# Decoding 64-bit weights with a sign-carrying parametric Relu and two VectorE passes

## The chip, the cores and the metric

The kernel runs on one core of a Trainium2 chip. The core has a matrix engine (TensorE, in the profile PE, with its weight loads as PEld), a vector engine (VectorE, DVE), an activation engine (ScalarE, ACT), a general engine (GpSimd, POOL) and a queue that starts transfers (SyncE, SP). Each engine works through its own instructions in the order in which the program lists them; between engines, semaphores hold an instruction back until its inputs are there or its output buffer is free.

The metric is the device time of one execution in microseconds (us). Lower is better.

## What is computed

Causal attention with a decay, over 8 batches, 8 heads, 576 tokens and 64 features a head, and then a two-layer block with a layer norm over the 512 features of each token:

```python
scores = scale * q @ k^T                       # scale = 1/8
scores = where(causal, -1e9, scores + cum[:, :, :, None] - cum[:, :, None, :])
attn   = softmax(scores) ; x = (attn @ v)      # heads side by side: 512 features
xn     = (x - mean) / sqrt(var + 1e-6) * g_ln
out    = x + maximum(xn @ w_ch1, 0) @ w_ch2    # 512 -> 2048 -> 512
```

`cum` is the running sum of log(f). The two weight matrices arrive as 64-bit floating point, 512 x 2048 and 2048 x 512; all else is 32-bit. The kernel reads a weight's 64 bits as two 32-bit words and makes a 32-bit number of them on the chip.

## The kernel before

**Work on attention.** The 64 heads are taken one after the other, each in four units (slots `t` = 1 to 4), 256 units in all. A unit runs the product of queries and keys (`qk_mm`, L368 to L371), a fused mask and minimum on VectorE (L394), the exponential on ScalarE (L405), a sum's reciprocal on VectorE (L410, L411) and a scaling on GpSimd (L412). Two units later the probabilities are transposed on TensorE (L418) and copied out (L468, and L473 on VectorE); a unit after that they are multiplied with the values (`av_unit`, L481 for the first 16 heads, L503 later) and finished on ScalarE (L534, L537). The first 8 heads use plain 32-bit products; from head 8 on, a head's raw queries and keys come through one buffer `raw` (L319), are rounded on ScalarE (L337, L344) and have the rest subtracted on GpSimd (L340, L348).

**The two-layer block.** Tokens are taken in 18 chunks of 256, each in 16 steps. A step is 12 products for the first layer (`mm1`, L580 to L582), a Relu on ScalarE (L588), a rest on VectorE (L593), and 6 products for the second layer (`mm2`, L602 to L604). The first step may run from unit 35 on, when the tokens and the weights that it reads are there. Each weight is used as a rounded part and a remainder (`w1h`, `w1l`, `w2h`, `w2s`).

**The preparation of the weights** is the class `WPrep`, where the change lies. There are 32 items, alternately a 512 x 128 block of the first matrix and a 128 x 512 block of the second; each is 512 words of 64 bits in each of 128 partitions. A tick starts the next item and moves the earlier ones on by a step:

- `load` (L143): a transfer into `raw` (tile `wr`, three buffers). The high words `hw` are every second 32-bit word, the low words `lw` the others.
- `scaled` (L156): ScalarE reads the high word as a 32-bit float and multiplies it by 2^-112, so that its exponent fits after a shift to the left by three. The result is the tile `wy` (five buffers).
- `decode` (L165): three VectorE steps. L173 keeps the sign bit of the high word, in place. L174 shifts `wy` left by three and sets the sign. L177 shifts the low word right by 29 and sets its three bits in `wy`.
- `colsum` (L182, first layer only, two ticks later): eight products (L189) that sum over features, for the mean of the layer norm; `centre` (L191): four VectorE steps (L197), one tick after that, which apply `g_ln` and subtract the mean.
- `high` (L211): ScalarE rounds (L214); `low` (L216): GpSimd subtracts (L218) and so frees the `wy` buffer; `keep` (L220): the second layer's remainders go out to memory.

**What sets the order.** The order of all instructions is written out by hand. A unit runs the pieces named by the letters of a string, for units 0 to 36 `WwQsSthAeMrgFBmlLNPaRf`, for 37 to 69 `WwQSstAMhPelgLNFrfmBRa`. "W" calls `tick` if one is due: about every 2.4 units up to unit 34, then 0.95 a unit, so that the items are done at about unit 57. A tick first runs whatever VectorE steps are left in the queue (`fill(99)`), then issues the loads and the steps `high`, `keep` and `low` of earlier items, and then puts the new item's decode steps and an older item's centring steps into the queue in turn. The scaling of the next item is put at place 5 of the queue, or at its end if it is shorter. Letters "w", "g" and "f" take 1, 2 and 3 entries out of the queue. A tick with a first-layer item (even) has no centring; one with a second-layer item (odd) has four centring steps. "Q" is the product of queries and keys, "e" the exponential, "r" the Relu, "F" the finish copy, "P" the preparation of the next head, "M" and "N" the two layers, "s" the column sums.

Of the kernel before, what the change touches and what calls it, by code (L numbers as in the profile page):

```python
# [8 lines left out]
F32 = mybir.dt.float32  # L9
# [3 lines left out]
AF = mybir.ActivationFunctionType  # L13
ALU = mybir.AluOpType
# [44 lines left out]
def attn_moe(ctx: ExitStack, tc: tile.TileContext, qk, v, f, g, w1, w2, out):  # L59
    nc = tc.nc  # L60
# [14 lines left out]
    def m2(name, dt):  # L75
        return work.tile([P, 512], dt, tag="m2", bufs=11, name=name)
# [9 lines left out]
    for i in range(WARM):  # L86
# [4 lines left out]
        out=mask[:, S - P :], in_=mask[:, S - P :], pattern=[[-1, P]], base=0,  # L91
# [42 lines left out]
    class WPrep:  # L134
# [21 lines left out]
        def scaled(self, n):  # L156
            layer, j = self.items[n]
            d = self.d[n]
            if layer == 1 and self.tick_no < W_BORROW:
                d["y"] = m2(f"wy{layer}_{j}", U32)  # L160
            else:
                d["y"] = wpool.tile([P, DM], U32, tag="wy", bufs=W_FLOAT, name=f"wy{layer}_{j}")
            nc.scalar.activation(d["y"].bitcast(F32), d["hw"].bitcast(F32), AF.Copy, scale=2.0**-112)

        def decode(self, n):  # L165
            layer, j = self.items[n]
            d = self.d[n]
            y, z, low = d["y"], d["hw"], d["lw"]
            d["w"] = y.bitcast(F32)
            ve = nc.vector  # L170

            return [
                lambda: ve.tensor_scalar(out=z, in0=z, scalar1=0x80000000, scalar2=None, op0=ALU.bitwise_and),  # L173
                lambda: ve.scalar_tensor_tensor(  # L174
                    out=y, in0=y, scalar=3, in1=z, op0=ALU.logical_shift_left, op1=ALU.bitwise_or
                ),
                lambda: ve.scalar_tensor_tensor(  # L177
                    out=y, in0=low, scalar=29, in1=y, op0=ALU.logical_shift_right, op1=ALU.bitwise_or
                ),
            ]  # L180

# [483 lines left out]
    class Moe:  # L665
# [21 lines left out]
        low = []  # L687
# [211 lines left out]
```

## Time and profile before

| | us |
|---|---|
| three runs | 1252.57, 1253.7, 1260.37 |
| their median | 1253.7 |
| span of the profiled execution, first to last instruction | 1260.6 |
| TensorE busy in it | 1230.2 |
| VectorE busy in it | 782.8 |
| ScalarE busy in it | 645.2 |
| GpSimd busy in it | 426.8 |

The profile is one execution recorded by the hardware. Its page gives the busy time of each engine, the same in 40 equal slices of the span together with the granted clock of TensorE, the chain of work that ended last (followed back from the last instruction: what released each step), and groups of instructions by line and tile, with the mean time of one and the idle time of the engine ahead of them. Further views give windows of time, single instructions in order of time, and waits by pairs of lines. In a row, `wy<-wy,wr` means that the tile `wy` is written from `wy` and `wr`; "L177" is line 177. Idle time of an engine that does not set the end costs nothing.

### The profile page before, as it was taken

The page shows a single profiled execution, that of the slowest core. Times are in us where ns is not written, and L with a number is a line of the kernel's source. Part 1 is how long each engine was busy: PE and PEld are TensorE (multiplying, and loading weights), DVE is VectorE, ACT ScalarE, POOL GpSimd, SP SyncE. Part 2 cuts the span into 40 slices and gives each one's busy share as a digit, 9 for nine tenths or more (in the row PEclk, how much of TensorE's full clock was granted, in tenths as well). Part 3 has the DMA queues.
Part 4 walks back from the last instruction along what each step waited for, and adds up shares of the span by engine and source line. Part 5 has one row for each costly group of instructions (what it writes and reads, how often), then busy time and mean ns, then how long its engine had stood idle before and what let it go on. Part 6 is the DMA issues. An engine that isn't in the chain of part 4 may idle for free.

```text
span 1260.6 us, 25515 instructions
## 1 busy us (share of the span) xinstructions
PE 1230.2 (98%) x8148; PEld 1085.2 (86%) x8148; DVE 782.8 (62%) x2868; ACT 645.2 (51%) x1920; POOL 426.8 (34%) x529
## 2 busy tenths in 40 slices
PE   8997898999999999999999999999999999999998
PEld 5554686889999999999999999999999999999997
DVE  5587888357576768576767666666767673233232
ACT  5577666555555556565656555655555552112111
POOL 3356556333343334334443434343434330000000
PEclk7799899999999999999999999999999999999999
DMA  5366674544554545444545454545454534444432
GB/s 154 110 183 204 198 240 160 159 124 155 154 165 148 168 141 171 137 150 149 156 144 160 145 168 151 168 151 166 149 152 147 168 104 136 125 126 117 151 109 92
DMA packets 139381, 190.77 MB, mean 151 GB/s; under 512 B 32496, under 2 KB 81648, under 8 KB 139248
## 3 DMA queue, kind: packets, MB, share of 16 engines
q1 hardware_dynamic: 139248, 189.15, 49.0%
q8 instruction: 65, 1.06, 0.3%
q14 instruction: 68, 0.56, 0.1%
HBM read 157.46 MB, written 23.36 MB: 143 GB/s over the span
## 4 chain that ended last, share of the span: by engine, by line
PE 86%; DVE 5%; DMA 4%; ACT 1%; POOL 1%; issue 1%; SPq 0%; DVEq 0%; POOLq 0%; ACTq 0%
PE h L580 11%; PE h L581 10%; PE h L582 10%; PE acc L602 10%; PE acc L603 10%; PE acc L604 10%; PE tr L418 7%; PE o L503 5%; PE o L481 3%; PE s L370 3%; PE s L371 3%; DMA raw<-in_qk_dram 3%; PE s L368 1%; PE xp L418 1%; DVE wy L174 1%
## 5 line engine op out<-in xcount | busy, mean ns | idle before, releaser
L412 POOL TENSOR_SCALAR p<-p,st 64x64 f32<-64x64 f32 (+4 forms) x320 | 173.8, 546 | 568.1 <-DVE st L411 225.9
L580 PE MATMUL h<-x,w1h 128*128 128x256 f32 x1152 | 329.6, 286 | 0.0
L581 PE MATMUL h<-x,w1h 128*128 128x256 f32 x1152 | 325.9, 283 | 0.7 <-DVE x L565 0.7
L582 PE MATMUL h<-x,w1l 128*128 128x256 f32 x1152 | 324.9, 282 | 0.0
L588 ACT ACTIVATE hh<-h 128x256 fp32r<-128x256 f32 x288 | 110.4, 383 | 287.7 <-PE h L582 281.0
L593 DVE SCALAR_TENSOR_TENSOR hh<-h,hh 128x256 fp32r<-128x256 f32 x288 | 121.4, 422 | 193.3 <-ACT hh L588 189.0
L602 PE MATMUL acc<-w2h,hh 128*128 128x512 f32 x576 | 228.1, 396 | 0.0
L603 PE MATMUL acc<-w2s,hh 128*128 128x512 f32 x576 | 226.4, 393 | 0.0
L604 PE MATMUL acc<-w2h,hh 128*128 128x512 f32 x576 | 225.7, 392 | 0.0
L580 PEld LDWEIGHTS h<-x,w1h 128*128 128x128 f32 x1152 | 218.2, 189 | 5.2 <-issue 0.9
L581 PEld LDWEIGHTS h<-x,w1h 128*128 128x128 f32 x1152 | 218.2, 189 | 4.6 <-DVE x L565 1.3
L582 PEld LDWEIGHTS h<-x,w1l 128*128 128x128 f32 x1152 | 218.0, 189 | 0.0
L405 ACT ACTIVATE p<-p,st 64x64 f32<-64x64 f32 (+4 forms) x320 | 178.3, 558 | 60.8 <-DVE st L394 58.1
L468 ACT CAST ph<-tr 64x128 fp32r<-64x128 f32 (+4 forms) x384 | 108.6, 332 | 110.4 <-PE tr L418 82.6
L418 PE MATMUL tr<-identr,p 128*128 128x128 f32 (+1 forms) x896 | 143.7, 277 | 9.0 <-POOL p L412 4.7
L394 DVE CUSTOM_DVE_ANT_0 p<-s,mask 64x64 f32<-64x64 f32 (+4 forms) x320 | 130.3, 420 | 15.5 <-PE s L368 9.8
L418 PEld LDWEIGHTS tr<-identr,p 128*128 128x128 f32 (+1 forms) x896 | 102.9, 132 | 35.3 <-POOL p L412 9.1
L604 PEld LDWEIGHTS acc<-w2h,hh 128*128 128x128 f32 x576 | 108.2, 188 | 25.3
L473 DVE TENSOR_TENSOR ph<-tr,ph 64x192 fp32r<-64x192 f32 x192 | 57.8, 301 | 106.1 <-ACT ph L468 102.9
L602 PEld LDWEIGHTS acc<-w2h,hh 128*128 128x128 f32 x576 | 108.7, 189 | 13.4 <-issue 0.9
L603 PEld LDWEIGHTS acc<-w2s,hh 128*128 128x128 f32 x576 | 109.0, 189 | 12.3
L370 PE MATMUL s<-hi 128*64 128x64 f32 x336 | 109.8, 349 | 8.3 <-POOL hi L348 6.5
(81 smaller groups left out, 1848.4 us busy)
## 6 DMA issues: line engine op xcount, KB each, us to landing
w2s<-w2d SPq DMA_DIRECT2D x288, 256.0 KB
raw<-in_qk_dram SPq DMA_DIRECT2D x56, 576.0 KB
wr<-in_w_dram SPq DMA_DIRECT2D x32, 512.0 KB
vr<-in_v_dram SPq DMA_DIRECT2D x64, 160.0 KB
out_dram<-xt SPq DMA_DIRECT2D x36, 256.0 KB
xq<-hi SPq DMA_DIRECT2D x56, 144.0 KB
xa<-xs SPq DMA_DIRECT2D x32, 160.0 KB
w2d<-wl SPq DMA_DIRECT2D x16, 256.0 KB
```

The lines of the kernel that those rows point to most:

```text
L370: mm(sp, h.hi[:, 0, q0 : q0 + m], h.hi[:, 1, a:z], start=True, stop=False)
L394: nc.vector.tensor_tensor_reduce(out=pt[:m, a:z], in0=sp, in1=mask[:m, off + a : off + z], scale=-SCALE, scalar=3.0e38 if i == 0 else st[: ...
L405: nc.scalar.activation(pt[:m, :w], pt[:m, :w], AF.Exp, bias=st[:m, i : i + 1], scale=-1.0, accum_out=st[:m, 2:3])
L412: nc.gpsimd.tensor_scalar(out=pt[:m, :w], in0=pt[:m, :w], scalar1=st[:m, 3:4], scalar2=1.0, op0=ALU.mult, op1=ALU.mult)
L418: nc.tensor.transpose(out_, in_, ident[:m, :m])
L580: mm(ph, w1h[:, k, fs], c.x[k][:, 0, :], start=(k == 0), stop=False)
L581: mm(ph, w1h[:, k, fs], c.x[k][:, 1, :], start=False, stop=False)
L582: mm(ph, w1l[:, k, fs], c.x[k][:, 0, :], start=False, stop=(k == KT - 1))
L593: nc.vector.scalar_tensor_tensor(out=h[:, 1, :], in0=ph, scalar=0.0, in1=h[:, 0, :].bitcast(F32), op0=ALU.max, op1=ALU.subtract)
L602: mm(c.acc[i], h[:, 0, ts_], w2h[:, j, :], start=(j == 0), stop=False)
L603: mm(c.acc[i], h[:, 0, ts_], low, start=False, stop=False)
L604: mm(c.acc[i], h[:, 1, ts_], w2h[:, j, :], start=False, stop=(j == FT - 1))
```

## The change

ScalarE's scaling becomes a parametric Relu. For a positive high word it gives the same as before. For a negative one, the scaled value is multiplied by alpha = 2^32 as well, so the exponent is higher by 32. The shift to the left by three drops the sign bit and the two upper bits of the exponent, and the bit of the exponent worth 32 lands where the sign belongs: the sign is carried through. The mask of the sign (before L173) and its separate combining pass (before L174) go. The shift of the low word by 29 becomes a pass of its own, in place, and one pass shifts `wy` and combines. An item has two VectorE decode steps in place of three; the queue and its letters are unchanged, so the later entries move up by one.

```diff
-            nc.scalar.activation(d["y"].bitcast(F32), d["hw"].bitcast(F32), AF.Copy, scale=2.0**-112)
+            nc.scalar.activation(d["y"].bitcast(F32), d["hw"].bitcast(F32), AF.Prelu, scale=2.0**-112, alpha=2.0**32)
...
-            y, z, low = d["y"], d["hw"], d["lw"]
+            y, low = d["y"], d["lw"]
...
-                lambda: ve.tensor_scalar(out=z, in0=z, scalar1=0x80000000, scalar2=None, op0=ALU.bitwise_and),
+                lambda: ve.tensor_scalar(out=low, in0=low, scalar1=29, scalar2=None, op0=ALU.logical_shift_right),
                 lambda: ve.scalar_tensor_tensor(
-                    out=y, in0=y, scalar=3, in1=z, op0=ALU.logical_shift_left, op1=ALU.bitwise_or
-                ),
-                lambda: ve.scalar_tensor_tensor(
-                    out=y, in0=low, scalar=29, in1=y, op0=ALU.logical_shift_right, op1=ALU.bitwise_or
+                    out=y, in0=y, scalar=3, in1=low, op0=ALU.logical_shift_left, op1=ALU.bitwise_or
                 ),
```

## The prediction

> **What bounds the kernel now.** I read the head of the page first, then a table of busy times by stage, then the chain of the work that ended last, stage by stage, and last the waits and the timeline where the chain leaves TensorE.
>
> ```profile
> span 1260.6 us, 25515 instructions
> PE 1230.2 (98%) x8148; PEld 1085.2 (86%) x8148; DVE 782.8 (62%) x2868; ACT 645.2 (51%) x1920; POOL 426.8 (34%) x529
> ...
> PE   8997898999999999999999999999999999999998
> ...
> DVE  5587888357576768576767666666767673233232
> ...
> PEclk7799899999999999999999999999999999999999
> ...
> PE 86%; DVE 5%; DMA 4%; ACT 1%; POOL 1%; issue 1%; SPq 0%; DVEq 0%; POOLq 0%; ACTq 0%
> ```
>
> TensorE is busy 98% and carries 86% of the chain. Only in the first seven slices (31.5 us each) is its line or its clock below the rest, and there the DVE line is highest. The weights are decoded in just that time. The next view is a table of windows: for each stretch its length, then busy us (and instructions) of PE, PEld, DVE, ACT, POOL, then the granted clock, the DMA share and GB/s.
>
> ```profile
> 0.00:14.00 14.00, 9.01 (x45) 7.61 (x45) 9.07 (x20) 6.14 (x10) 5.74 (x15) 0.99 0.66 198
> 14.00:44.00 30.00, 29.97 (x88) 18.79 (x89) 14.74 (x56) 14.44 (x44) 8.17 (x13) 0.50 0.41 108
> 44.00:98.00 54.00, 50.77 (x249) 31.37 (x248) 40.30 (x151) 38.56 (x121) 26.05 (x32) 0.96 0.56 167
> 98.00:138.00 40.00, 27.12 (x138) 17.95 (x137) 29.85 (x84) 25.00 (x72) 25.89 (x26) 0.87 0.59 179
> 138.00:180.00 42.00, 42.00 (x275) 35.35 (x273) 38.46 (x98) 27.77 (x76) 24.39 (x23) 1.00 0.72 227
> 180.00:220.00 40.00, 35.71 (x225) 28.19 (x224) 32.39 (x108) 25.05 (x71) 23.19 (x25) 1.00 0.59 190
> 220.00:1260.00 1040.00, 1035.66 (x7139) 945.91 (x7138) 618.00 (x2358) 508.21 (x1527) 313.34 (x397) 1.00 0.48 146
> ```
>
> After 220 us TensorE idles 4.3 us in 1040: whatever is won earlier is kept there, and nothing more is won. In 138 to 180 it idles not at all, though DVE is busy 38.46 of 42 us. In 14 to 44 it is busy throughout at half the clock. What a lighter DVE can still take away is TensorE's idle time: 3.2 us in 44 to 98, 12.9 in 98 to 138 and 4.3 in 180 to 220, together 20.4 us, and some at the very start.
>
> **The change part by part.** The rows by form give count, busy us, mean ns, and idle time ahead.
>
> ```profile
> L163 ACT ACTIVATE wy<-wr 128x512 f32<-128x512 f32 x32 | 21.5, 671 | 8.3 <-POOL w1l L218 3.6 <-DMA wr<-in_w_dram 2.7 <-POOL wl L218 1.9
> ...
> L173 DVE TENSOR_SCALAR wr<-wr 128x512 uint32<-128x512 uint32 x32 | 16.9, 528 | 0.8 <-ACT wy L163 0.8
> ...
> L174 DVE SCALAR_TENSOR_TENSOR wy<-wy,wr 128x512 uint32<-128x512 uint32 x32 | 35.3, 1103 | 0.0
> ...
> L177 DVE SCALAR_TENSOR_TENSOR wy<-wr,wy 128x512 uint32<-128x512 uint32 x32 | 30.2, 945 | 0.6
> ```
>
> (a) *The scaling* stays one ACTIVATE on the same 512 words. No Prelu is in this trace. Nearest is the Copy that it replaces, 671 ns; a gain is excluded since the same words go through the same engine, and the far end is a reload of the activation table (a rival below). I take 671, so nothing. (b) *The mask of the sign* (L173) goes and *the shift of the low word* comes: one tensor_scalar in place on the other strided half of the same tile. I take the row of L173 for both, so nothing. It now waits for the load and no longer for ScalarE, and the load is one that the scaling of the same item awaited before it. (c) *One of two combining passes goes*: the new one has the shape and strides of L174, so L177's row is what is saved. 32 x 945 ns = 30.2 us of DVE, 35.3 us by L174's row.
>
> ```profile
> 115.60 1.41 POOL L340 TENSOR_TENSOR kl<-raw,hi 64x576 fp32r<-64x576 f32 x1
> ...
> 115.95 1.62 DVE L174 SCALAR_TENSOR_TENSOR wy<-wy,wr 128x512 uint32<-128x512 uint32 x1
> ...
> L177 DVE SCALAR_TENSOR_TENSOR wy<-wr,wy x32: 676/693/1807, 9.0 to 203.5; 128x512 uint32<-128x512 uint32 x32
> ```
>
> The third row has min, median and max: 676, 693 and 1807 ns. Two rows above, a pass that began 0.35 us after a POOL operation ended 0.56 us after it: the long ones lie beside POOL. That time may pass on to the pass that is left, so the low end is 32 x 676 ns = 21.6 us. I take the rows of the chain below for the path and these for the load. The Trainium skill says the same against the change: by "SBUF — State Buffer", the section "Who interferes with whom", a DVE operation with two SBUF inputs and a POOL operation that reads SBUF lock each other out for a whole instruction. By that rule the wait belongs to POOL's work and stays, and the saving is nearer 21.6 us than 30.2.
>
> What lies on the path: the lines of the chain in three of these stages.
>
> ```profile
> by line: PE o L481 13.3%; DMA raw<-in_qk_dram 10.8%; DVE wy L174 10.3%; DMA kl<-in_qk_dram 7.6%; DVE wy L177 6.8%; DVE p L394 6.6%; PE s L368 6.1%; ACT p L405 6.1%; POOL p L412 5.9%; issue 5.6%; PE tr L418 4.2%; POOL w1l L218 3.4%; DVE wr L
> ...
> by line: DMA raw<-in_qk_dram 39.0%; issue 13.1%; PE o L481 10.6%; POOL hi L348 7.6%; POOL p L412 5.7%; DVE x L565 4.2%; ACT ph L468 3.6%; POOL kl L340 3.5%; DVE wy L197 3.5%; ACT p L405 3.5%; DVE wy L177 3.1%; POOL w1l L218 2.3%; PE tr L418
> ...
> by line: DMA wr<-in_w_dram 13.3%; PE o L481 9.9%; DMA xr<-xb 9.2%; DVE wy L174 9.1%; DVE wr L173 8.1%; DVE wy L177 5.2%; DVE wy L197 4.2%; PE acc L602 3.5%; PE tr L418 3.5%; DVE p L394 3.4%; issue 2.9%; PE h L582 2.5%; PE h L580 2.5%; PE h
> ```
>
> L177 has 6.8% of 53 us (45 to 98) = 3.6 us, 3.1% of 39 us (98 to 137) = 1.2 us, and 5.2% of 38 us (180 to 218) = 2.0 us. The pieces of the chain in order of time (start, us, what) show it where it counts:
>
> ```profile
> 53.91 1.64 DVE wy L177
> ...
> 69.31 0.69 DVE wy L177
> ...
> 82.03 0.69 DVE wy L177
> ...
> 194.38 0.60 DVE wy L177
> ...
> 199.69 0.69 DVE wy L177
> ...
> 203.47 0.68 DVE wy L177
> ```
>
> TensorE idles only 3.2 us in the first stage, so between 0 and 3.2 I take three passes of 0.68 = 2.0 there: behind them TensorE's own matmuls are late next. In the third stage the three pieces are 1.97, under its 4.3 us of idle time. In the second the loads of raw, 39% of 39 us = 15.2 us, are late next. In 138 to 180, TensorE covers all of it; if that cover were gone, some 8 passes of 0.68 to 0.95 us would show.
>
> ```profile
> ACT w1h L214 <- DVE wy L197: 17.2, 9, 3.6
> ...
> PE s L370 <- POOL hi L348: 6.5, 2, 3.7
> ...
> PE tr L418 <- DVE wy L197: 4.1, 1, 4.1
> ```
>
> (Total us, times, longest.) (d) *The queue of VectorE steps gets shorter.* On ticks with a centring (odd), the steps were two decode steps each beside a centring step, the third, the scaling, and two centrings flushed at the next tick; now one is flushed. The rounding w1h at that next tick waits 17.2 us in 9 places for the last centring. One pass and one centring fewer ahead of it shorten some of these waits; off the path they cost nothing. Between 0 (ScalarE is not the bound) and 9 x 0.95 = 8.6 us, I take 0.8 us in 98 to 138 and 0.5 us in 180 to 220, near the low end, since ACT holds 1% of the chain.
>
> ```profile
> 9.88 2.11 PE L368 MATMUL s<-kl,xf 66*64 66x64 f32 x8 [1.36 <-DMA kl<-cumr]
> ...
> 12.15 0.69 DVE L177 SCALAR_TENSOR_TENSOR wy<-wr,wy 128x512 uint32<-128x512 uint32 x1
> ...
> 13.64 1.03 PE L418 MATMUL tr<-identr,p 128*64 128x128 f32 x3 [1.65 <-POOL p L412]
> ```
>
> (e) *The start.* L177 of item 1 stands ahead of the softmax's small VectorE steps; TensorE's wait of 1.65 us shortens by its 0.69 us, 0.7, and stage 14 to 44 begins that much sooner.
>
> (f) *The scaling of the next item moves forward on even ticks.* With two decode steps instead of three it leaves with fill "g" and not with "f", ahead of the finish copy and of the raw halves. No DMA is issued anew, and SP's order stays. It waits today 8.2 us in all (3.6 + 2.7 + 1.9 in its row above). Gain excluded: its result is needed a tick later; a loss up to a POOL subtraction on each of 16 ticks (rival). I take 0, as the seven waits there now are mostly under 1.2 us (8.2 / 7).
>
> **Sum**: 2.0 + 1.2 + 2.0 + 0.8 + 0.5 + 0.7 = 7.2 us off 1260.6, 0.57%. The profiled execution stands 0.55% above the median of the three runs, 1253.7, near the slowest, 1260.4. Off the median: 1246.5, say 1247.
>
> **The rivals.**
> *Hidden anyway.* TensorE is full in 14 to 44 and 138 to 180, and in 98 to 138 the loads of raw end last. Then only the 0.7 of the start and a little of 180 to 220 stay: about 1252. Against it stands DVE's unbroken part of the chain around 191 to 205 us.
>
> *The clock is kept.*
>
> ```profile
> 123.00:126.00 3.00, 3.00 (x11) 0.50 0.88 271
> ...
> 130.00:136.00 6.00, 4.09 (x11) 0.50 0.53 153
> ```
>
> (TensorE alone: length, busy, clock, DMA share, GB/s.) After gaps TensorE runs at half clock: 30 us after the two gaps at the start, 3 and 6 us later. If the shorter second gap keeps the clock up, stage 14 to 44 falls from TensorE's 30 us to DVE's: 14.74 us at the 75% load that DVE has in 44 to 98 (40.30 / 54) = 19.8 us. That saves 10 more: 1236. Against it: the first gap stays, and the gap left is still about 1 us. "TensorE: Matmul & The Clock Gate" of the Trainium skill, in Part 1, has the clock return after one busy window of about 3.4 us. The trace differs: 29.97 busy us at 0.50.
>
> *Slower, by the moved scaling.*
>
> ```profile
> L218 POOL TENSOR_TENSOR wl<-wy,w2h x16: 1265/1362/1701, 38.1 to 212.3; 128x512 fp32r<-128x512 f32 x16
> ```
>
> Each of 16 even ticks could hold ScalarE for the subtraction that frees the buffer, 16 x 1.36 = 21.8 us; less 7.2 that is +14.6: 1268. It decides only if nearly all reaches TensorE, 19.7 us of 21.8 for over 1%. For it: two waits on wl are there now. Against: ACT is idle 83 of the first 220 us.
>
> *Slower, by table reloads.*
>
> ```profile
> L114 ACT ACT_TABLE_LOAD x1 | 1.3, 1283 | 0.7 <-PEq L887 0.7
> L405 ACT ACT_TABLE_LOAD x1 | 1.3, 1283 | 0.0
> ```
>
> Two loads in all, at Ln and at the first Exp; Copy and Relu run between exponentials without one. If Prelu were not in the table of Exp, each item would need two: 64 x 1.283 = 82 us. ACT's 137 us up to 220 (the six rows above) become 219; at the 92% load that DVE reaches in 138 to 180 they need 238: +18, 1272. The Trainium skill, "ScalarE: Activation LUTs", section on table sets, puts cheap functions such as relu and copy in every set, without naming Prelu.
>
> **How the numbers follow.** Forecast 0.48, hidden 0.25, clock 0.20, moved scaling 0.04, tables 0.03. A measurement here tells about 1% (12.5 us) from no change. Faster by over 1%: the clock and 0.02 of the forecast's upper end, 0.22. Slower: the last two, 0.07. Within: 0.71. The range reaches from the clock's 1236 to 1257, above the hidden case by the spread of the runs; 0.07 above and some below are left out. The forecast's own range is 1241 to 1251.
>
> **What would show it.** Right: L177's group gone, 32 instructions fewer on DVE, DVE busy in 44 to 220 down by 18 to 28 us; two table loads; the scaling near 671 ns; TensorE idle in 180 to 220 under 2.5 us; the chain at 191 to 205 without 0.7 us per item. Wrong: stage 98 to 138 still 40 us long with DVE lighter (then raw's load is the bound); ScalarE's waits at the scaling well over 8.2 us; another clock in 14 to 44.

## The result and the profile after

The changed kernel takes 1248.17 us (median of 20 runs, 1241.18 to 1255.70) against 1254.32 us before (20 runs, 1250.38 to 1268.25). The ratio is 0.9936, with a 95% interval from 0.9911 to 0.996: some 5 to 11 us faster, 0.6%, inside the 1% that was called no change. The forecast was 1247.

The page of the changed kernel, head, slices and chain:

```profile
span 1241.2 us, 25467 instructions
PE 1221.9 (98%) x8148; PEld 1081.0 (87%) x8148; DVE 751.8 (61%) x2836; ACT 646.4 (52%) x1920; POOL 425.5 (34%) x529
...
PE   8998999999999999999999999999999999999998
...
DVE  5666676366676767676767586767667663233232
...
PEclk8997999999999999999999999999999999999999
...
PE 88%; DVE 3%; ACT 3%; DMA 2%; POOL 2%; issue 1%; SPq 1%; POOLq 0%; DVEq 0%; ACTq 0%
```

VectorE lost 32 instructions and 31.0 us of work (782.8 to 751.8) and holds 3% of the chain instead of 5%. The span is 19.4 us shorter, three times what the medians say. The table by stage (length, then busy us and instructions of PE, PEld, DVE, ACT, POOL, then granted clock, DMA share, GB/s) shows why:

```profile
0.00:14.00 14.00, 9.26 (x49) 7.70 (x50) 6.80 (x18) 6.26 (x10) 5.68 (x16) 0.93 0.67 195
14.00:44.00 30.00, 28.94 (x140) 18.36 (x138) 19.04 (x84) 22.16 (x70) 12.59 (x19) 0.92 0.64 173
44.00:98.00 54.00, 50.94 (x239) 31.96 (x239) 33.29 (x140) 38.76 (x123) 28.39 (x37) 0.90 0.60 180
98.00:138.00 40.00, 35.14 (x196) 27.24 (x196) 29.00 (x88) 27.48 (x77) 24.90 (x24) 0.88 0.67 209
138.00:180.00 42.00, 41.13 (x260) 33.18 (x258) 28.56 (x88) 27.06 (x73) 25.77 (x24) 1.00 0.71 229
180.00:220.00 40.00, 39.53 (x246) 31.36 (x245) 25.14 (x98) 25.72 (x79) 20.38 (x23) 1.00 0.55 175
```

In this execution the stage from 14 to 44 us ran at a clock of 0.92, with 140 matmuls done; the profiled execution before had 0.50 and 88. The two profiles differ in the change and in the clock, and cannot be subtracted. TensorE's idle time from 44 to 220 us fell from 20.4 to 9.3 us (3.06 + 4.86 + 0.87 + 0.47), in windows that no longer hold the same work: the last column sum, at 202.6 us before, is at 185.1 now.

**Runs at the same clock.** Each run of the changed kernel and of all that follow lists its time and its mean granted clock, and the two go together: in every kernel here runs with a lower mean clock tend to take longer. A line through the runs of all kernels below, with one slope and a level for each kernel, has a slope of 9.7 us for each 0.01 of clock and leaves a scatter of 1.9 us. Four runs with a mean clock under 0.965 are left out of it: three slow ones (1693.7 us at 0.654 in e5, 1695.4 at 0.652 in the kernel before, 1989.7 at 0.555 in e9) and one of e8, 1253.9 us at 0.938, which lies far off the line. The level at a clock of 0.988 compares kernels without that lottery: 1254.6 +- 0.4 us before (93 runs), 1247.6 +- 0.8 after, a difference of 7.1 +- 0.9.

The 93 runs of the kernel before are those beside the experiments, on three chips, with a level of 1254.5 to 1254.8 on each; the 20 beside the changed kernel list no clock. The level takes out whatever a change does through the clock itself. The mean clock was 0.986 before and 0.987 after, a difference of 0.0018 +- 0.0025, so a share of 1.7 +- 2.4 us by that way is neither shown nor excluded. The table gives this level beside medians and ratios; the ratio's interval holds the clock's scatter, the level's does not.

| kernel | runs | median us | ratio to before (95%) | mean clock | level at 0.988, us |
|---|---|---|---|---|---|
| changed | 20 | 1248.2 | 0.9936 (0.9911 to 0.996) | 0.987 | 1247.6 +- 0.8 |
| e1, parametric Relu alone | 12 | 1257.1 | 1.0011 (0.9981 to 1.0041) | 0.984 | 1254.6 +- 1.1 |
| e2, empty third entry | 8 | 1246.4 | 0.9924 (0.9893 to 0.9954) | 0.988 | 1247.5 +- 1.3 |
| e3, three passes in two entries | 12 | 1258.5 | 1.0022 (0.999 to 1.0055) | 0.981 | 1253.8 +- 1.1 |
| e4, pass put back | 12 | 1257.2 | 0.9995 (0.9968 to 1.0021) | 0.986 | 1254.8 +- 1.1 |
| e5, changed, start filled | 8 | 1247.4 | 0.9905 (0.9868 to 0.9941) | 0.989 | 1248.2 +- 1.4 |
| e6, before, start filled | 12 | 1256.0 | 0.9982 (0.9948 to 1.0016) | 0.988 | 1255.5 +- 1.1 |
| e7, changed, raw split | 9 | 1247.0 | 0.9906 (0.9869 to 0.9943) | 0.987 | 1245.9 +- 1.2 |
| e8, before, raw split | 12 | 1252.2 | 0.996 (0.9928 to 0.9991) | 0.987 | 1251.2 +- 1.1 |
| e9, changed, filled and split | 12 | 1245.4 | 0.9899 (0.9865 to 0.9934) | 0.990 | 1246.0 +- 1.1 |
| e10, pass back in items 0 to 12 | 12 | 1247.4 | 0.9948 (0.9917 to 0.998) | 0.988 | 1250.1 +- 1.1 |
| e11, pass back in items 13 to 19 | 12 | 1249.1 | 0.9937 (0.9903 to 0.997) | 0.988 | 1248.9 +- 1.1 |
| e12, pass back in items 20 to 31 | 12 | 1251.1 | 0.9961 (0.9934 to 0.9989) | 0.986 | 1249.1 +- 1.1 |

The mean clock is that of the runs on the line. Ratios are to the runs of the kernel before on the same chip, whose median was 1256.9 beside e1 to e4, 1257.6 beside e5 to e8 and 1254.9 beside e9 to e12.

The rows by form of the changed kernel (count, busy us, mean ns, idle time ahead) answer to those of the decode; the centring is now L194, the rounding L211, the subtraction L215, the load of raw L316 and its remainder L345:

```profile
L163 ACT ACTIVATE wy<-wr 128x512 f32<-128x512 f32 x32 | 21.4, 668 | 10.4 <-POOL w1l L215 3.5 <-POOL wl L215 3.4 <-DMA wr<-in_w_dram 3.3
...
L174 DVE SCALAR_TENSOR_TENSOR wy<-wy,wr 128x512 uint32<-128x512 uint32 x32 | 35.9, 1121 | 0.1
...
L173 DVE TENSOR_SCALAR wr<-wr 128x512 uint32<-128x512 uint32 x32 | 14.9, 464 | 0.0
```

The scaling costs what it did (668 ns after 671). The pass that stays is about as long as the like one before (1121 after 1103), and the one of 945 ns is gone. The shift of the low word takes 464 ns where the mask took 528.

### The profile page after: what moved, and what is told of

The parts are those of the page before. It is cut to its first block, busy times and chain, and to the rows that moved or that the text cites. A ratio compares the mean times of both kernels' runs of the same rounds, so it can differ in the third digit from the quotient of the medians.

```text
span 1241.2 us, 25467 instructions
## 1 busy us (share of the span) xinstructions
PE 1221.9 (98%) x8148; PEld 1081.0 (87%) x8148; DVE 751.8 (61%) x2836; ACT 646.4 (52%) x1920; POOL 425.5 (34%) x529
## 4 chain that ended last, share of the span: by engine, by line
PE 88%; DVE 3%; ACT 3%; DMA 2%; POOL 2%; issue 1%; SPq 1%; POOLq 0%; DVEq 0%; ACTq 0%
PE h L577 11%; PE h L578 11%; PE h L579 11%; PE acc L599 10%; PE acc L600 10%; PE acc L601 10%; PE tr L415 7%; PE o L500 5%; PE s L367 3%; PE s L368 3%; PE o L478 3%; DMA raw<-in_qk_dram 2%; PE xp L415 1%; PE s L365 1%; ACT p L402 1%
```

## The experiments

**e1: the parametric Relu alone.** All three VectorE passes stay; the sign is then set twice, to the same value.

```diff
-... AF.Copy, scale=2.0**-112)
+... AF.Prelu, scale=2.0**-112, alpha=2.0**32)
```

> The kernel before with only the scaling turned into the parametric Relu; the mask and both combining passes stay (the sign is set twice, to the same value). If the gain comes from the VectorE pass that goes (my theory), this is the kernel before: 1254, ratio 0.997 to 1.003, two table loads, the scaling at 671 ns within 2%. If the parametric Relu itself costs or saves something on ScalarE, the ratio leaves that band, and the scaling's mean or the count of table loads shows it.

Measured: 1.0011 (0.9981 to 1.0041). ScalarE's rows by form:

```profile
L163 ACT ACTIVATE wy<-wr 128x512 f32<-128x512 f32 x32 | 21.5, 672 | 8.5 <-POOL w1l L218 3.6 <-DMA wr<-in_w_dram 2.9 <-POOL wl L218 1.9
...
L114 ACT ACT_TABLE_LOAD x1 | 1.3, 1283 | 0.7 <-PEq L887 0.7
...
L405 ACT ACT_TABLE_LOAD x1 | 1.3, 1283 | 0.0
```

672 ns, and two table loads in all, as before: the table that holds the exponential holds this function too. The parametric Relu costs and saves nothing that shows; it only makes the pass superfluous.

**e2: the changed kernel with the queue as before.** An empty third entry; the scaling of the next item and the centring leave the queue where they did before.

```diff
                 lambda: ve.scalar_tensor_tensor(
                     out=y, in0=y, scalar=3, in1=low, op0=ALU.logical_shift_left, op1=ALU.bitwise_or
                 ),
+                lambda: None,
```

> The changed kernel with an empty third entry in the queue, so that every other entry, the scaling of the next item among them, leaves the queue where it did before; only the pass is gone. Theory (the pass itself): the whole gain stays, ratio about 0.994. Rival (the entries moved up, which shortens the wait of the rounding for the last centring): the gain is gone or halved, 0.997 to 1.0. Third possibility, the moved scaling costs something: this is faster than the changed kernel, under 0.992.

**e3: the kernel before with the queue as after.** The two combining passes in one entry.

```diff
-                lambda: ve.scalar_tensor_tensor(... in1=z, ...),
-                lambda: ve.scalar_tensor_tensor(... in0=low, scalar=29, in1=y, ...),
+                combine,          # both passes, one after the other
```

> The kernel before, all three passes kept, but the two combining passes in one entry of the queue, so that the order of all other work is that of the changed kernel. Theory (the pass itself): no gain, ratio 0.997 to 1.003. Rival (the order): most of the gain, about 0.995. If the moved scaling costs: slower than before, over 1.003.

Measured: e2 0.9924 (0.9893 to 0.9954), level 1247.5, the whole gain; e3 1.0022 (0.999 to 1.0055), level 1253.8, no gain. The order of the queue, with the scaling moved forward on even ticks, does nothing that shows. The rounding's wait for the last centring, in the rows by form of e2 and then of e3, is 9.3 us with two passes in the old order, though two centrings are still flushed with the next tick, and 17.6 us with three passes in the new order:

```profile
L212 ACT CAST w1h<-wy 128x512 fp32r<-128x512 f32 x16 | 9.8, 615 | 9.3 <-DVE wy L195 9.3
...
L217 ACT CAST w1h<-wy 128x512 fp32r<-128x512 f32 x16 | 9.8, 616 | 17.7 <-DVE wy L200 17.6
```

The kernel before has 17.2 us and the changed one 8.5. So that wait shrank by the missing pass, not by the order.

**e4: the pass put back.** A third pass of the same shape, strides and inputs, which changes nothing.

```diff
+                lambda: ve.scalar_tensor_tensor(
+                    out=y, in0=low, scalar=0, in1=y, op0=ALU.logical_shift_right, op1=ALU.bitwise_or
+                ),
```

> The changed kernel with a third VectorE pass put back that changes nothing (the low word, shifted by nothing, combined into the result again): same shape, strides and inputs as the pass that went, and the queue as it was. Theory: back at the kernel before, ratio 0.998 to 1.002, VectorE busy 30 us more than in the changed kernel. If the gain came from the scaling or from the shift's freedom to start ahead of ScalarE, part of it stays: 0.995 to 0.998.

Measured: 0.9995 (0.9968 to 1.0021): all of the gain is given back. e2 and e4 also help to read the two profiles, since the clock's draw in them was the other way round. The head of e2's page and its rows of the table by stage:

```profile
span 1254.1 us, 25469 instructions
...
PE 1229.9 (98%) x8148; PEld 1084.7 (86%) x8148; DVE 756.2 (60%) x2836; ACT 644.9 (51%) x1920; POOL 422.5 (34%) x529
```

```profile
14.00:44.00 30.00, 29.35 (x87) 18.17 (x86) 11.97 (x54) 14.53 (x45) 7.07 (x12) 0.50 0.42 111
44.00:98.00 54.00, 51.52 (x263) 31.97 (x261) 36.30 (x150) 41.63 (x130) 26.95 (x36) 1.00 0.64 187
98.00:138.00 40.00, 31.33 (x169) 22.80 (x167) 27.95 (x86) 25.61 (x75) 25.07 (x27) 0.87 0.64 196
138.00:180.00 42.00, 42.00 (x269) 34.99 (x269) 31.81 (x92) 27.53 (x75) 25.10 (x23) 1.00 0.72 226
180.00:220.00 40.00, 38.23 (x236) 29.65 (x235) 25.50 (x95) 27.15 (x80) 24.18 (x26) 1.00 0.55 173
```

And e4's:

```profile
span 1248.0 us, 25504 instructions
...
PE 1220.6 (98%) x8148; PEld 1078.7 (86%) x8148; DVE 782.8 (63%) x2868; ACT 644.4 (52%) x1920; POOL 427.3 (34%) x529
```

```profile
14.00:44.00 30.00, 28.61 (x142) 18.33 (x142) 21.92 (x83) 21.59 (x68) 12.80 (x19) 0.94 0.62 171
44.00:98.00 54.00, 48.17 (x238) 29.45 (x236) 39.86 (x151) 38.25 (x118) 29.99 (x37) 0.97 0.56 167
98.00:138.00 40.00, 33.02 (x181) 24.49 (x181) 32.41 (x91) 27.05 (x78) 23.28 (x25) 0.87 0.66 201
138.00:180.00 42.00, 41.53 (x264) 34.08 (x263) 38.14 (x94) 26.16 (x72) 25.19 (x24) 1.00 0.74 229
180.00:220.00 40.00, 37.21 (x233) 29.63 (x232) 28.65 (x100) 25.49 (x76) 22.70 (x24) 1.00 0.55 175
```

VectorE's work in e4 is that of the kernel before, 782.8 us. Now compare like with like. At half clock from 14 to 44 us, three passes take 1260.6 (the kernel before) and two take 1254.1: 6.5 us. At nearly full clock, three take 1248.0 and two 1241.2: 6.8 us. TensorE's idle time from 44 to 220 us falls by about as much, from 20.4 to 12.9 us in the first pair and from 16.1 to 9.3 in the second. So the gain is found again as idle time that TensorE no longer has. The clock of these 30 us goes with 12.6 us (1260.6 - 1248.0) or 12.9 (1254.1 - 1241.2), twice as much as the change. Each figure is of one execution: e1, with three passes and 0.50 in this stage, took 1262.3 us, 1.7 more than the kernel before.

**e5 and e6: the gaps at the start filled**, in the changed kernel and in the one before. The transposes write a buffer that nobody reads.

```diff
-WARM = 36
+WARM = 44
...
                 qk_mm(h, t)
+                if u == 0:
+                    more = bank("more")
+                    for i in range(10):
+                        nc.tensor.transpose(more[:, 0:P], ident, ident)
```

> The changed kernel with more TensorE work in its two gaps at the start: 8 more warm-up transposes, and 10 transposes of the identity behind the first unit's product of queries and keys. They write nothing that is used. Theory: the gaps decide whether 14 to 44 us runs at half clock, and that stage decides most of the spread of the runs (some 12 us). Then the granted clock in 14 to 44 is near 1.0, the runs fall together near 1243, and the median is 1241 to 1245, ratio 0.985 to 0.991. Rival: the clock falls for another reason. Then the spread stays (1241 to 1256) and the median is that of the changed kernel or up to 2 us longer for the added work, 0.993 to 0.996.

> The same fill in the kernel before. Theory: its gain from the clock is the same, so it comes to 1247 to 1252, ratio 0.991 to 0.996, and stays 6 to 8 us behind the changed kernel with the fill. Rival (the change won because its shorter start gap keeps the clock more often): with the fill in both, the two kernels are alike within 2 us.

Measured: 0.9905 (0.9868 to 0.9941) and 0.9982 (0.9948 to 1.0016), levels 1248.2 and 1255.5. With the same fill in both, the change is still worth 7.3 us at the same clock, and 8.6 between the medians at mean clocks of 0.989 and 0.988: it does not win by keeping the clock. The fill did not win what was expected of it. The medians were to be 1241 to 1245 and 1247 to 1252 and are 1247.4 and 1256.0, and neither level is below that of the same kernel without the fill. The row of the stage, e5 and then e6:

```profile
14.00:44.00 30.00, 28.05 (x132) 17.28 (x131) 18.34 (x79) 21.53 (x67) 10.77 (x17) 0.89 0.61 169
```

```profile
14.00:44.00 30.00, 27.31 (x141) 17.01 (x142) 21.94 (x83) 21.54 (x68) 12.76 (x18) 1.00 0.62 171
```

In e6's profiled execution the two gaps were down to 0.19 and 0.56 us and the stage ran at full clock. In e5's a gap of 1.09 us ahead of the first product was left, and the clock was 0.89, no better than the 0.92 without the fill. Seven of e5's runs lie within 1245.6 to 1250.1, but e6's still spread from 1248.7 to 1259.9. So filling these gaps does not take the spread away, and its cause stays open.

**e7 and e8: raw split** into a tile for keys and one for queries, in the changed kernel and in the one before. The keys' tile comes free after the unit `t` = 2, the queries' after 3.

```diff
-        h.raw = late.tile([P, 2, S], F32, tag="raw", bufs=1, name=f"raw{n}")
-        nc.sync.dma_start(out=h.raw, in_=qk[n])
+        h.rk = late.tile([P, S], F32, tag="rk", bufs=1, name=f"rk{n}")
+        h.rq = late.tile([P, S], F32, tag="rq", bufs=1, name=f"rq{n}")
+        nc.sync.dma_start(out=h.rk, in_=qk[n][:, 1, :])
+        nc.sync.dma_start(out=h.rq, in_=qk[n][:, 0, :])
...
```

> The changed kernel with raw split into a tile for keys and one for queries, each loaded on its own; the keys' tile comes free a unit earlier. Theory: in 80 to 125 us and in 180 to 220 the loads of raw end last once VectorE is lighter, so this wins 1 to 5 us more: ratio 0.989 to 0.993, and TensorE's wait for the remainder of raw and ScalarE's for its load fall. Rival: the load is not on the path, or the second transfer costs as much in SP's queue: 0.993 to 0.996.

> The same split in the kernel before. If VectorE and the loads share the path before the change, the split wins less here than in the changed kernel: 0.997 to 1.000. If the loads are the bound whatever VectorE does, it wins as much: 0.993 to 0.997.

Measured: 0.9906 (0.9869 to 0.9943) and 0.996 (0.9928 to 0.9991). At the same clock the split wins 1.7 +- 1.5 us in the changed kernel, where the ratios with and without it overlap, and 3.4 +- 1.2 in the one before. The loads of raw are on the path, then, but that the split would win more once VectorE is lighter is not borne out. The waits from 8 to 220 us (total us, times, longest), in the changed kernel and in e7:

```profile
ACT hi L334 <- DMA raw<-in_qk_dram: 6.4, 4, 2.4
...
PE s L367 <- POOL hi L345: 2.9, 2, 2.3
```

```profile
ACT hi L336 <- DMA rk<-in_qk_dram: 4.1, 3, 1.8
...
PE s L369 <- POOL hi L347: 4.6, 2, 2.5
```

ScalarE's wait for the load fell, as expected. TensorE's wait for the remainder of raw was to fall too and did not, in one execution of each.

**e9: both edits in the changed kernel.**

> The changed kernel with both edits at once: the filled start gaps and raw split in two. Theory: they act in different stages and add up, each about 3 us over the changed kernel's ratio of 0.9936: 0.985 to 0.990, the runs within 5 us of each other. Rival: what the one wins the other finds already hidden: 0.990 to 0.992.

Measured: 0.9899 (0.9865 to 0.9934), median 1245.4 and fastest run 1237.6, the fastest of all kernels. It beats the kernel before clearly; against e5, e7 and the changed kernel the intervals overlap, and its level (1246.0) is e7's (1245.9). That the two edits add up is not shown. The runs were to lie within 5 us of each other; those on the line spread from 1237.6 to 1251.8.

**e10, e11, e12: the pass put back in one stretch of items each**, by a condition on `n` around e4's pass.

> The changed kernel with the idempotent third pass put back for items 0 to 12 only (up to about 98 us in the profile before). By the terms of the forecast (start 0.7, second stage 2.0) it loses 2.7 us against the changed kernel; by the markers in the traces (head 8's raw starts 3.6 to 5.2 us earlier without the pass) it loses 4 to 5, some 1252 to 1253.

> The third pass put back for items 13 to 19 only (98 to 138 us in the profile before). Forecast's terms: loses 2.0 us. Markers (the stretch from head 8's raw to the first product of the two-layer block is 1.2 to 3.0 us shorter without the pass): loses 1 to 3. Where this loses nothing, the loads of raw hide it there.

> The third pass put back for items 20 to 31 only (from 138 us on). Forecast's terms: loses 2.5 us, the largest but one. Markers (from the first product of the two-layer block to the last column sum and to head 16 the two kernels take the same within 1 us): loses 0 to 0.5, since TensorE and the loads of raw carry that stretch.

Measured at the same clock, against the changed kernel: 2.5, 1.3 and 1.5 us lost, each +- 1.4; the sum is 5.3 +- 3 of 7.1. The items without the pass keep an empty entry in the queue, as in e2, whose level is the changed kernel's. The ratios alone (0.9948, 0.9937, 0.9961) overlap with each other and with the changed kernel's. So no one stretch is shown to hold the whole gain; that each holds a part is likely, but the losses of e11 and e12 are about as large as their intervals. The markers were a poor guide: e10 was to lose 4 to 5 us by them and e12 no more than 0.5. Between one profiled execution and another these stretches vary by more than the terms: from the first product of the two-layer block to the last column sum it is 65.6 us in the kernel before, 64.9 in e4 and 68.2 in e3, all with three passes.

## Why the prediction was right

The total was right in mechanism and size: 7.2 us forecast, 7.1 +- 0.9 at the same clock, 6.2 between the medians. The mechanism is the one that was named: VectorE has one pass fewer for each item, and TensorE idles less in the stages where it had waited for such passes (e4, e2). That the two totals meet within 0.1 us is in part luck, since the terms behind the sum came out less well than the sum. Its steps:

- **(a) and the rival of table reloads.** Nothing was forecast for the parametric Relu, and e1 shows nothing. The reload did not come: e1 has the same two table loads.
- **(b), (c) The passes.** The saving of VectorE's work was put between 21.6 and 35.3 us and taken as 30.2; it was 31.0 in the changed kernel's profile and 26.6 in e2's. In the first, 2.0 of it are the shift of the low word, which took 14.9 us where the mask took 16.9 and for which nothing was forecast; in e2 it took 16.9. The low end held that the time beside GpSimd's work would pass on to the pass that is left. Most of it did not: that pass has 1121 ns where it had 1103, and 1140 in e2. The weighed rule of the Trainium skill ("SBUF — State Buffer", "Who interferes with whom") would have put the saving nearer 21.6, and the measurement decides against this use of it. Of the 64 combining passes before, 32 took over 0.8 us, each of them beside a GpSimd operation; of the 32 now, 22 do.
- **(d) The queue.** The rounding's wait for the last centring halved, but by the missing pass and not by the entries that moved up: e2 keeps the order of before and has the short wait and the whole gain, e3 has the new order and neither. As a step of its own, worth 1.3 us, the shorter queue failed; what the shorter wait is worth apart from the pass is not measured.
- **(e) The start.** TensorE's gap ahead of the first transposes, in the timeline of the changed kernel:

```profile
9.88 2.11 PE L365 MATMUL s<-kl,xf 66*64 66x64 f32 x8 [2.25 <-DMA kl<-cumr]
...
11.02 0.69 DVE L174 SCALAR_TENSOR_TENSOR wy<-wy,wr 128x512 uint32<-128x512 uint32 x1
...
12.51 1.03 PE L415 MATMUL tr<-identr,p 128*64 128x128 f32 x3 [0.52 <-POOL p L409]
```

The transposes start 1.13 us sooner (13.64 to 12.51) where 0.7 was forecast: 0.7 is the pass that stood ahead of the softmax's small steps, and 0.4 comes from the softmax's first VectorE step (10.41 us, before 11.01), since the tensor_scalar ahead of it now runs at 8.96 us in 0.42 us, where the mask began at 9.62, behind the third pass of item 0, and took 1.26 us. The gap behind the warm-up, ahead of the first product, is set by a load and was 2.25 us here and 1.36 before. That the end comes sooner by these 1.13 us is not shown; e10 holds them together with the stage to 98 us.

- **(f) and the rival of the moved scaling.** The scaling's waits rose from 8.3 to 10.4 us. In e2, with the scaling where it was, they are 9.6, so its move is not the whole of that rise, and no loss of time by it shows (e3, e2).
- **The terms by stage.** Forecast 2.7 (start and up to 98 us), 2.0 and 2.5; measured 2.5, 1.3 and 1.5, each +- 1.4. None is refuted, and the division is only coarsely tested.
- **Hidden anyway** fell: 7.1 is not 2. **The clock is kept** fell as the reason for the gain (e2 and e4 at unlike clocks, e5 and e6 with the fill), though the runs of one kernel, which differ by up to 19 us (e3: 1252.97 to 1272.08), go with the granted clock.

What was said would show it: the group of L177 is gone, and VectorE's work from 44 to 220 us fell from 141.0 to 116.0 us, inside the 18 to 28 less. TensorE idles 0.5 us from 180 to 220, under 2.5. As the changed kernel is 17 us ahead by then, e2 is the fairer test of both, with the same half clock as before: 121.6 us, 19.4 less, and 1.8 us. Of the signs of being wrong, another clock in 14 to 44 us did come up; it is not tied to the change, since e2 has two passes at 0.50 and e4 three at 0.94. The waits in question (total us, times, longest, 8 to 220 us):

```profile
ACT w1h L211 <- DVE wy L194: 8.5, 8, 2.3
...
PE s L367 <- POOL hi L345: 2.9, 2, 2.3
...
PE tr L415 <- DVE wy L194: 1.2, 1, 1.2
```

They were 17.2, 6.5 and 4.1. Only the first can be put down to the pass: it is 9.3 in e2 and 16.7 in e4. The second is 5.5 in e2, with two passes, and 4.8 in e4, with three; the third is 1.6 and 2.4. What is late next in the changed kernel's profile are the loads of raw, as forecast for 98 to 138 us, and later too. Pieces of its chain between 160 and 205 us, the part of the program in which VectorE's passes stood in the chain before:

```profile
165.72 6.46 DMA raw<-in_qk_dram
...
184.09 5.08 DMA raw<-in_qk_dram
```

In e2 the chain of that part holds no load of raw, but loads of weights and of token rows and VectorE's remaining pass; so which work is late next differs between executions.

Of the 31.0 us taken off VectorE, 24 did not come back as time: they lay beside TensorE's own work and beside loads.

## What to carry to other kernels

An engine that is busy 62% on the whole can hold a chain for 14 us at a time; what lightening it is worth is bounded by the idle time of the bounding engine in just those stretches, here 20 us of 1260 and a little at the start, and came to a third of it. Before two profiles are subtracted, compare the granted clock stage by stage, and if it differs, pair each with a run of a near-identical kernel that drew the same clock; a fit of time against mean clock over all runs narrowed a difference of 7 us from +- 3 to +- 1, though it leaves out what the change may do to the clock. To split a gain between "less work" and "another order", keep the one and undo the other in both directions.

## What was not expected of the hardware

After two gaps of 1.4 and 1.7 us, TensorE ran at half clock for 30 us though it was busy all the time (29.97 of 30 us at 0.50); in other executions of nearly the same program the same stage ran at 0.92 to 1.00. The Trainium skill ("TensorE: Matmul & The Clock Gate", Part 1) has the full clock return after one busy window of about 3.4 us; later in the same trace stretches of 3 and 6 us agree with it better, this one does not. The length of the gaps does not decide it here: e3 had longer ones (2.10 and 2.08 us) and ran at full clock again from 20 to 36 us, e7 had shorter ones (1.18 and 0.51) and a clock of 0.77 in the stage, and e11 with about e7's gaps (1.26 and 0.51) ran at full clock all through it. What does is open.
